# Sliding attention and a GEGLU block on one core: attention instructions over two token tiles, low weight parts by adding DMAs, kept x operands, weight loads issued by GpSimd

## The chip, the cores and the metric

The kernel runs on one core of a Trainium2 chip. The metric is the device time of one execution in microseconds (us). Five engines work from queues of their own: TensorE (PE) for matmuls, VectorE (DVE), ScalarE (ACT), GpSimd (POOL), and SyncE (SP), which here only issues DMAs. Each engine takes its instructions in order.

## The reference

With 2048 tokens, D = 512, 32 heads of 16, a feed-forward width of 1792 and all values in float32:

```
q, k, v = split(x @ wqkv)                      # 32 heads of 16
logits[s, w] = q[s] . k[s - 2 w] / 4           # w = 0..7; positions before 0 masked
a = (softmax(logits) @ v[s - 2 w]) @ wo
b = (gelu(x @ w_gate) * (x @ w_up)) @ w_down   # tanh form of gelu
g = sigmoid(sum(x * gate_w))
out = g * a + (1 - g) * b
```

## The kernel before

**Precision.** PE multiplies in float32r. Each operand is split into a high part (ACT copies it into float32r) and a low part, the raw value minus the high part; three products (high-high, high-low, low-high) replace one. The helper `split` (L64 to L69) does this: the copy at L68, the subtraction at L69, on whichever engine it is given.

**Parities.** A token only attends to tokens of its own parity, so the tokens are dealt into even and odd (`par` 0 and 1), 1024 each, in 8 tiles (`NP`) of 128.

**Projection.** `load_cb` brings in wqkv columns in three blocks (`cb`), `load_xk` and `load_x1` bring in x, and `project` multiplies them for each parity (L177). ACT or DVE evicts PSUM (`take`, L187, L189), and SP stores q, k and v to DRAM (`ks`, `qs`, `vs`).

**Attention** is DVE work. A generator, `attention`, goes through 8 units (parity, then 8 heads each), and in each through `scores`, `softmax` and `mix`. `scores` multiplies, tile by tile, 8 shifted k rows with q into `prod` (L238, 1024 elements per partition) and sums over the 16 values of a head (L239). POOL masks the result with `affine_select` (L242), for which `softmax` waits. `mix` multiplies v with the weights (L273), then folds 8 rows to one in three additions (L277, L278, L279) and transposes four tiles (L283); SP stores that to DRAM as `os`. The generator yields a cost after each group of instructions, and `pull(budget)`, called between pieces of the matrix work, draws as much as its budget allows. So these costs and budgets, and then a scheduler that reorders within dependencies, decide where attention stands between the other instructions of DVE.

**FFN.** For each parity, 14 chunks of 128 hidden columns (`FC`, loop in `ffn`). `gate_up` computes gate and up of two token blocks by seven products instead of eight, from sums of x blocks (`s1` to `s4`, made by `sums`, L114 to L117) and sums of weight blocks (`t1` to `t4`, made by `combine` at L344). The names `a11`, `a12`, `a22` are x blocks, `b11`, `b21`, `b22` weight blocks. `product` (L381) issues six matmuls. ACT and DVE take the results out (L385, L390, L466, L482), `hidden` multiplies gelu(gate) with up (L394) and splits (L396, L397; the subtraction is DVE's in parity 0 and POOL's in parity 1). `down` (L420) multiplies with w_down, two chunks at a time, one group behind.

**Weights of the FFN.** In parity 0, `fetch` loads a chunk's gate and up weights into `raw` from SP, `combine` makes the sums on DVE, and `operands` splits seven 256-column blocks into `w` tiles (ACT copy, POOL subtraction), each stored to DRAM as `ws`. `down_w` does the same for w_down (`d`, stored as `ds`). In parity 1 both are loaded back ready-made (`w<-ws`, `d<-ds`) by SP.

**x of the second parity.** At the end of parity 0's FFN, `operands_1` loads x again and makes sums and splits for the FFN of parity 1, with POOL doing the subtractions. `finish` multiplies attention's output, read back by `channels` in four DMAs per half, with wo (L557), scales and stores.

Tiles of `pool` with the same name share a fixed number of buffers (`BUFS`); a new tile waits until the readers of the oldest are done.

Of the kernel before, what the change touches and what calls it, by code (L numbers as in the profile page):

```python
# [33 lines left out]
OPS = ("b11", "t1", "t2", "b21", "b22", "t3", "t4")  # L34
# [3 lines left out]
def tile_gated_mix(ctx: ExitStack, tc: tile.TileContext, xt, wqkv, wff, wo, out):  # L38
# [6 lines left out]
    BUFS = {"A": 16, "S": 16, "w": 14, "d": 4, "raw": 2, "t": 1, "hh": 6, "hl": 6, "c": 4, "s": 3,  # L45
            "r": 2, "rt": 4, "p": 4, "lg": 2}
    COLS = {"w": 2 * WQ, "c": 2 * WQ, "d": 1024, "t": 1024, "raw": WT}

    def tl(tag, dt=F32):
        return pool.tile([P, COLS.get(tag, 512)], dt, name=tag, bufs=BUFS[tag])  # L50

# [20 lines left out]
    KS, VS, QS, OS, WS, DS = {}, {}, {}, {}, {}, {}  # L72
    for par in range(2):
        for hh in range(2):
            for n, t in (("k", KS), ("v", VS)):
                t[par, hh] = dram.tile([2, W + S // 2, UC], F32, name=f"{n}s{par}{hh}")
                for c in range(2):
                    nc.gpsimd.dma_start(t[par, hh][c, :W], zero)
            QS[par, hh] = dram.tile([2, S // 2, UC], F32, name=f"qs{par}{hh}")
        for u in range(NU):  # L80
            for half in range(2):
                OS[par, u, half] = dram.tile([32, 4, BT * P], F32, name=f"os{par}{u}{half}")


    early = iter(["c", "rt"] * 99)
    X, WC = {}, {}

    def load_xk(kc, blk, first=False):
        hi, lo = tl("A", F32R), tl("A", F32R)
        X[0, blk, kc] = hi, lo  # L90
        for a, n in ((0, P), (P, 512 - P)) if first else ((0, 512),):
            raw = tl(next(early))
# [4 lines left out]
    def load_cb(cb, kc, eng, tag=None):  # L97
        hi, lo = tl("w", F32R), tl("w", F32R)
        WC[cb, kc] = hi, lo
        raw = tl(tag or "c")  # L100
        if cb == 1:
            n = 2 * WQ
            for hh in range(2):
                nc.sync.dma_start(raw[:, hh * WQ:(hh + 1) * WQ], wqkv[hh, 2, :, kc * WQ:(kc + 1) * WQ])
        else:
            n = 512
            nc.sync.dma_start(raw[:, :n], wqkv[cb // 2, kc // 2, :, kc % 2 * 512:kc % 2 * 512 + 512])
        return lambda: split(eng, hi[:, :n], lo[:, :n], raw[:, :n])

    def sums(par, kc, a, b, eng, put, eng2=None):  # L110

        t = tl("t")
        s1, s2, s3, s4 = t[:, :512], t[:, 512:], b[:, :512], a[:, 512:1024]
        eng.tensor_tensor(s1, b[:, :512], b[:, 512:1024], op=OP.add)  # L114
        eng.tensor_tensor(s2, s1, a[:, :512], op=OP.subtract)
        eng.tensor_tensor(s3, a[:, :512], b[:, :512], op=OP.subtract)
        eng.tensor_tensor(s4, a[:, 512:1024], s2, op=OP.subtract)  # L117
        for n, s in (("s1", s1), ("s2", s2), ("s4", s4), ("s3", s3)):
            hi, lo = tl("S", F32R), tl("S", F32R)
            split(eng2 or eng, hi, lo, s)  # L120
            put(n, hi, lo)
            yield

    def raw_pair(par, kc):
        ab = []
        for blk in range(2):
            raw = tl("raw")
            nc.sync.dma_start(raw[:, :1024].rearrange("p (a c) -> p a c", a=2), xt[2 * par + blk, :, kc:kc + 3:2, :])
            ab.append(raw)
        return ab  # L130

    XOP, nxt = {}, {}

    def load_x1():
        for kc in range(2):
            a, b = raw_pair(1, kc)
            for blk, raw in ((0, a), (1, b)):
                for i in range(2):
                    if blk == 1 and (kc, i) != (1, 1):
                        d = tl("d", F32R)  # L140
                        hi, lo = d[:, :512], d[:, 512:]
                    else:
                        hi, lo = tl("hh", F32R), tl("hl", F32R)
                    X[1, blk, kc + 2 * i] = hi, lo
                    split(nc.vector, hi, lo, raw[:, i * 512:(i + 1) * 512])

    def operands_0():
        for kc in range(2):
            a, b = raw_pair(0, kc)
            for _ in sums(0, kc, a, b, nc.vector, lambda n, hi, lo: XOP.__setitem__((n, kc), (hi, lo))):  # L150
                pass
# [3 lines left out]
    def operands_1(first):  # L155
        for kc in range(2):
            a, b = raw_pair(1, kc) if kc else first
            for n, raw in (("a11", a[:, :512]), ("a12", a[:, 512:1024]), ("a22", b[:, 512:1024])):
                nxt[n, kc] = tl("A", F32R), tl("A", F32R)
                split(nc.gpsimd, *nxt[n, kc], raw)  # L160
                yield
            yield from sums(1, kc, a, b, nc.vector, lambda n, hi, lo: nxt.__setitem__((n, kc), (hi, lo)), nc.gpsimd)
# [69 lines left out]

    def scores(par, u):
        k, q = LG[par, u]
        lg = pool.tile([P, NP, W, UH], F32, name="lg", bufs=2)
        for jj in range(NP):
            prod = pool.tile([P, W, UC], F32, name="prod")
            nc.vector.tensor_tensor(prod, k[:, jj:jj + W, :], q[:, jj, None, :].to_broadcast([P, W, UC]), op=OP.mult)  # L238
            nc.vector.tensor_reduce(lg[:, jj].rearrange("p w h -> p (w h)"),  # L239
                                    prod.rearrange("p w (h d) -> p (w h) d", d=DH), axis=AX.X, op=OP.add)  # L240
            yield 2.5
# [21 lines left out]
    def mix(par, u):  # L263
# [4 lines left out]
        tb = pool.tile([P, NP, UC], F32, name="tb")  # L268
        for jj in range(NP):
            if jj % BT == 0:  # L270
                o = pool.tile([P, BT, UC], F32, name="o")
            prod = pool.tile([P, W, UC], F32, name="prod")
            nc.vector.tensor_tensor(prod.rearrange("p w (h d) -> p w h d", d=DH),  # L273
                                    v[:, jj:jj + W, :].rearrange("p w (h d) -> p w h d", d=DH),
                                    lg[:, jj, :, :, None].to_broadcast([P, W, UH, DH]), op=OP.mult)
            yield 1.2
            nc.vector.tensor_tensor(prod[:, :4], prod[:, :4], prod[:, 4:], op=OP.add)  # L277
            nc.vector.tensor_tensor(prod[:, :2], prod[:, :2], prod[:, 2:4], op=OP.add)  # L278
            nc.vector.tensor_tensor(o[:, jj % BT], prod[:, 0], prod[:, 1], op=OP.add)  # L279
            yield 1.4  # L280

            if jj % BT == BT - 1:
                nc.vector.transpose(tb[:, jj + 1 - BT:jj + 1].rearrange("p t c -> p (t c)"),  # L283
                                    o.rearrange("p t c -> p (t c)"))
                for a in range(4):
                    nc.sync.dma_start(OS[par, u, jj // BT][:, a], tb[32 * a:32 * a + 32, jj + 1 - BT:jj + 1])
# [44 lines left out]
    RAW = {}  # L331

    def fetch(f):
        raw = tl("raw")
        nc.sync.dma_start(raw[:, :1024], wff[f, :, :1024])
        RAW[f] = [raw]

    def combine(f):

        raw, t = RAW[f][0], tl("t")  # L340
        quart = raw[:, :1024].rearrange("p (a b) -> p a b", a=4)
        b11, b21, b12, b22 = (raw[:, i * 256:(i + 1) * 256] for i in range(4))
        t1, t3, t2, t4 = (t[:, i * 256:(i + 1) * 256] for i in range(4))
        sub = lambda o, a, b: nc.vector.tensor_tensor(o, a, b, op=OP.subtract)  # L344
        sub(t[:, :512].rearrange("p (a b) -> p a b", a=2), quart[:, 2:], quart[:, 0::2])
        sub(t2, b22, t1)
        sub(t4, b21, t2)
        RAW[f] = dict(b11=b11, b21=b21, b22=b22, t1=t1, t2=t2, t3=t3, t4=t4)

    def operands(par, f):  # L350

        WG[f] = {}
        if not par:
            WS[f] = dram.tile([len(OPS), P, 512], F32, name=f"ws{f}")
        for n in OPS if par else ("t1", "t2", "t3", "t4", "b11", "b21", "b22"):
            i = OPS.index(n)
            w = WG[f][n] = tl("w", F32R)
            if par:
                nc.sync.dma_start(w[:, :512].bitcast(F32), WS[f][i])
            else:  # L360
                split(nc.gpsimd, w[:, :256], w[:, 256:512], RAW[f][n])
                nc.sync.dma_start(WS[f][i], w[:, :512].bitcast(F32))
            yield

    def down_w(par, f):
        d = WD[f] = tl("d", F32R)
        if par:
            nc.sync.dma_start(d.bitcast(F32), DS[f])
            return
        rd = tl("r")  # L370
        nc.sync.dma_start(rd, wff[f, :, 1024:])
        DS[f] = dram.tile([P, 1024], F32, name=f"ds{f}")
        split(nc.gpsimd, d[:, :512], d[:, 512:], rd)
        nc.sync.dma_start(DS[f], d.bitcast(F32))

    def product(ps, a, w, start):
        for kc in range(2):
            ah, al = XOP[a, kc]
            wh, wl = w[:, kc * P:(kc + 1) * P], w[:, 256 + kc * P:256 + (kc + 1) * P]
# [13 lines left out]
    def hidden(key, ge, up, eng):  # L393
        nc.vector.tensor_tensor(ge, ge, up, op=OP.mult)  # L394
        hh_, hl_ = tl("hh", F32R), tl("hl", F32R)
# [36 lines left out]
    def gate_up(par, f, steps):  # L432
# [14 lines left out]

        X_ = bank("p")
# [13 lines left out]
        piece()  # L462
        idle(0.5)
# [7 lines left out]
        piece()  # L471
        product(X_, "s3", w["t3"], False)
# [3 lines left out]
        piece()  # L476
        idle(0.0)
# [7 lines left out]

    def ffn(par):
        for f in range(FC):
            def more():
                if f + 1 < FC:
                    for i, _ in enumerate(operands(par, f + 1)):  # L490
                        if i == 4 and not par and f + 2 < FC:
                            combine(f + 2)
                        yield
                else:
                    yield from load_o((0, 1), "w")
# [160 lines left out]
```

## Time and profile before

| what | value |
|---|---|
| median of 3 runs (lowest to highest) | 679.92 us (678.1 to 680.22) |
| profiled execution, its own time | 680.39 us |
| its span | 678.6 us, so 1.79 us lie around it |
| PE busy | 631.2 us (93%), 2839 matmuls |
| DVE busy | 584.4 us (86%), 714 instructions |
| ACT busy | 313.8 us (46%), 601 instructions |
| POOL busy | 236.1 us (35%), 198 instructions |
| mean granted TensorE clock | 0.967 |
| DMA | 136.46 MB, 116046 packets, 42400 of them under 512 B |

Matmuls are pipelined, so PE counts as busy when it is not full; the count of matmuls in a stretch tells more. The profile has the chain of waits, groups of instructions by line and shape (count, busy time, mean time of one, idle time ahead of them and what ended it), and, for any stretch of time, the busy time of every engine.

### The profile page before, as it was taken

To read this page: it belongs to the slowest core of one execution; us is meant where nothing else is said; L and a number is where in the kernel's file an instruction comes from. 1 tells how busy PE (TensorE), PEld (TensorE's weight loads), DVE (VectorE), ACT (ScalarE), POOL (GpSimd) and SP (SyncE) were. 2 spreads that over 40 slices of the span, in tenths; PEclk is the share of its full clock that TensorE was granted. 3 is DMA by queue.
4 is the path that set the end of the run, shared out by engine and by line. 5 is a ranking of instruction groups with operands and counts; after the bars stand their busy time and mean duration, and the time that the engine had idled before them with its cause. 6 is when DMAs were issued, how large, how long until landed. Compare 5 with 4: busy or idle time off the path is not lost.

```text
span 678.6 us, 8894 instructions
## 1 busy us (share of the span) xinstructions
PE 631.2 (93%) x2839; PEld 512.9 (76%) x2839; DVE 584.4 (86%) x714; ACT 313.8 (46%) x601; POOL 236.1 (35%) x198
## 2 busy tenths in 40 slices
PE   8998999996799979997989849999999999999997
PEld 6888998874587758875868637888777888887785
DVE  5439899879999999989999988998999999989432
ACT  4424442245446455655454564234434644454562
POOL 5204014066737364634471760023122221224220
PEclk9999999998799989998998978999999999999999
DMA  8885755597966665675457587776566766544163
GB/s 254 269 253 172 247 156 187 172 300 250 310 235 218 243 229 171 234 252 208 156 191 224 159 225 158 249 234 218 179 187 197 214 196 197 185 124 127 36 104 124
DMA packets 116046, 136.46 MB, mean 201 GB/s; under 512 B 42400, under 2 KB 68640, under 8 KB 116000
## 3 DMA queue, kind: packets, MB, share of 16 engines
q1 hardware_dynamic: 115488, 135.84, 63.8%
q8 instruction: 22, 0.36, 0.2%
q14 instruction: 24, 0.20, 0.1%
q0 software_dynamic: 512, 0.07, 0.1%
HBM read 81.80 MB, written 54.07 MB: 200 GB/s over the span
## 4 chain that ended last, share of the span: by engine, by line
DVE 41%; PE 38%; DMA 7%; issue 6%; ACT 4%; SPq 1%; POOL 1%; DVEq 0%; POOLq 0%; ACTq 0%
PE p L381 21%; DVE prod L273 6%; PE p L420 6%; PE acc L420 5%; DVE prod L238 5%; DVE prod L277 4%; DVE lg L239 4%; DMA raw<-xt 4%; PE acc L557 3%; PE p L557 3%; DVE t L344 3%; DVE c L394 3%; DVE c L390 2%; DVE prod L278 2%; DVE o L279 2%
## 5 line engine op out<-in xcount | busy, mean ns | idle before, releaser
L381 PE MATMUL p<-S,w 128*128 128x512 f32 x672 | 176.6, 406 | 10.2 <-DVE c L390 4.1
L381 PEld LDWEIGHTS p<-S,w 128*128 128x128 f32 x672 | 130.8, 195 | 42.8 <-DVE c L390 4.5
L381 PE MATMUL p<-A,w 128*128 128x512 f32 x504 | 135.6, 407 | 16.2 <-DVE c L390 16.0
L381 PEld LDWEIGHTS p<-A,w 128*128 128x128 f32 x504 | 97.1, 194 | 42.4 <-DVE c L390 20.0
L397 POOL TENSOR_TENSOR hl<-c,hh 128x512 fp32r<-128x512 f32 x28 | 44.7, 1595 | 168.5 <-ACT hh L396 141.4
L238 DVE TENSOR_TENSOR prod<-k,q 128x1024 f32<-128x1024 f32 x64 | 86.8, 1356 | 11.5 <-DMA q<-qs 10.6
L273 DVE TENSOR_TENSOR prod<-v,lg 128x1024 f32<-128x1024 f32 x64 | 81.5, 1273 | 6.7 <-DMA v<-vs 5.3
L420 PE MATMUL p<-d,hh 128*128 128x512 f32 x224 | 71.7, 405 | 10.5 <-ACT p L414 10.4
L239 DVE TENSOR_REDUCE lg<-prod 128x64 f32<-128x1024 f32 x64 | 77.7, 1214 | 1.1
L69 POOL TENSOR_TENSOR w<-t,w 128x256 fp32r<-128x256 f32 x56 | 58.4, 1056 | 48.2 <-ACT w L68 38.5
L396 ACT ACTIVATE hh<-c 128x512 fp32r<-128x512 f32 x56 | 35.3, 631 | 80.3 <-DVE c L394 80.0
L69 POOL TENSOR_TENSOR w<-raw,w 128x256 fp32r<-128x256 f32 x42 | 43.0, 1034 | 63.8 <-ACT w L68 60.6
L277 DVE TENSOR_TENSOR prod<-prod 128x512 f32<-128x512 f32 x64 | 59.0, 922 | 1.3
L420 PEld LDWEIGHTS p<-d,hh 128*128 128x128 f32 x224 | 43.0, 194 | 22.0 <-ACT p L414 11.8
L420 PE MATMUL acc<-d,hh 128*128 128x512 f32 x224 | 57.7, 394 | 0.7 <-ACT hh L396 0.7
L420 PEld LDWEIGHTS acc<-d,hh 128*128 128x128 f32 x224 | 41.8, 188 | 11.7 <-ACT hh L396 2.4
L394 DVE TENSOR_TENSOR c<-c 128x512 f32<-128x512 f32 x56 | 44.6, 796 | 5.2 <-ACT c L482 4.8
L385 ACT ACTIVATE s<-p 128x512 f32<-128x512 f32 x56 | 32.8, 593 | 26.2 <-PE p L381 26.2
L390 DVE TENSOR_TENSOR c<-p,s 128x512 f32<-128x512 f32 x56 | 38.0, 681 | 8.0 <-PE p L381 7.8
L420 PE MATMUL p<-d,hl 128*128 128x512 f32 x112 | 42.9, 394 | 0.0
L429 ACT ACTIVATE rt<-p 128x512 f32<-128x512 f32 x48 | 28.6, 595 | 29.4 <-PE p L420 28.0
L177 PE MATMUL p<-w,A 128*128 128x512 f32 (+2 forms) x192 | 38.5, 345 | 2.9 <-ACT w L68 1.1
(125 smaller groups left out, 1002.0 us busy)
## 6 DMA issues: line engine op xcount, KB each, us to landing
ws<-w SPq DMA_DIRECT2D x98, 256.0 KB, 2.9
w<-ws SPq DMA_DIRECT2D x98, 256.0 KB, 2.7
raw<-wff SPq DMA_DIRECT2D x14, 512.0 KB, 5.0
ds<-d SPq DMA_DIRECT2D x14, 512.0 KB, 3.9
d<-ds SPq DMA_DIRECT2D x14, 512.0 KB, 4.5
raw<-xt SPq DMA_DIRECT2D x12, 512.0 KB, 5.4
k<-ks SPq DMA_DIRECT2D x8, 512.0 KB, 5.0
q<-qs SPq DMA_DIRECT2D x8, 512.0 KB, 6.3
```

What stands on the lines that cost most here:

```text
L69: eng.tensor_tensor(lo, raw, hi.bitcast(F32), op=OP.subtract)
L177: nc.tensor.matmul(ps[:, :cn], a[:, t], w[:, c0:c0 + cn], start=(kc == 0 and n == 0), stop=(kc == KC - 1 and n == 2))
L238: nc.vector.tensor_tensor(prod, k[:, jj:jj + W, :], q[:, jj, None, :].to_broadcast([P, W, UC]), op=OP.mult)
L239: nc.vector.tensor_reduce(lg[:, jj].rearrange("p w h -> p (w h)"), prod.rearrange("p w (h d) -> p (w h) d", d=DH), axis=AX.X, op=OP.add)
L273: nc.vector.tensor_tensor(prod.rearrange("p w (h d) -> p w h d", d=DH), v[:, jj:jj + W, :].rearrange("p w (h d) -> p w h d", d=DH), lg[:, ...
L277: nc.vector.tensor_tensor(prod[:, :4], prod[:, :4], prod[:, 4:], op=OP.add)
L381: nc.tensor.matmul(ps, w_, a_, start=(start and kc == 0 and n == 0), stop=(kc == 1 and n == 2), skip_group_check=True)
L390: nc.vector.tensor_tensor(c, ps, s, op=OP.add)
L394: nc.vector.tensor_tensor(ge, ge, up, op=OP.mult)
L397: eng.tensor_tensor(hl_, ge, hh_.bitcast(F32), op=OP.subtract)
L420: nc.tensor.matmul(pp, a[:, ts], w, start=(i == 0 and n == 0 and gr == 0), stop=(i == 1 and n == 2), skip_group_check=True)
L557: nc.tensor.matmul(pa, a, b, start=False, stop=(u == NU - 1 and n == 2), skip_group_check=True)
```

## The change

Four things are changed, and buffers are laid out anew to make room.

1. **Two token tiles per instruction.** `scores` and `mix` work on two tiles at once: `prod` has 2048 elements, a view `spans` reads the two overlapping sets of 8 rows. Costs in `yield` are new. `o`, `tb` and `os` are laid out so that `channels` reads a half with one DMA in whole rows.
2. **Low weight parts by adding DMAs.** `operands` lets ACT write the negated high part into the low part's place, and a DMA issued by GpSimd adds the raw value to it in SBUF; then ACT writes the high part. The seven blocks and an unused quarter lie in one `raw` tile, so that there are two such steps per chunk (768 and 1024 columns). `combine` works in place.
3. **Both parities make their weights.** `ws` and `ds` are gone; `fetch`, `combine`, `operands` and `down_w` run for every chunk of both parities. `fetch` (two DMAs), `fetch_d` and wo's `fetch_o` are issued by GpSimd. `ahead` and `again` prepare the first chunks of parity 1 while parity 0 ends.
4. **x operands of parity 1 are kept.** `load_x1` also makes the sums and their splits, on DVE, at the start; `keep` and `keep_x1` store all of them to DRAM, 28 DMAs from GpSimd, and `operands_1` loads each back at the end of parity 0, 14 DMAs from GpSimd. Parity 0's output is also stored by GpSimd.

The core of the diff:

```diff
+GROUPS = (("t1", "t2", "b11"), ("b22", "t3", "t4", "b21"))
+QUARTS = ("t1", "t2", "b11", "b12", "b22", "t3", "t4", "b21")
...
+    def keep(n, kc, hi, lo):
+        x = XS[n, kc] = dram.tile([P, 1024], F32, name=f"x{n}{kc}")
+        nc.gpsimd.dma_start(x[:, :512], hi.bitcast(F32))
+        nc.gpsimd.dma_start(x[:, 512:], lo.bitcast(F32))
...
+            for n, x in sums(a, b):
+                hi, lo = pair("S")
+                split(nc.vector, hi, lo, x)
+                keep(n, kc, hi, lo)
...
-        for jj in range(NP):
-            prod = pool.tile([P, W, UC], F32, name="prod")
-            nc.vector.tensor_tensor(prod, k[:, jj:jj + W, :], q[:, jj, None, :].to_broadcast([P, W, UC]), op=OP.mult)
...
-            yield 2.5
+        for jj in range(0, NP, 2):
+            prod = pool.tile([P, 2, W, UC], F32, name="prod")
+            nc.vector.tensor_tensor(prod, spans(k, jj), q[:, jj:jj + 2, None, :].to_broadcast([P, 2, W, UC]), op=OP.mult)
+            yield 2.3
...
+            yield 2.3
...
     def fetch(f):
-        raw = tl("raw")
-        nc.sync.dma_start(raw[:, :1024], wff[f, :, :1024])
-        RAW[f] = [raw]
+        raw = RAW[f] = tl("raw")
+        r = raw.rearrange("p (a c) -> p a c", c=QW)
+        q = wff[f, :, :1024].rearrange("p (a c) -> p a c", c=QW)
+        nc.gpsimd.dma_start(r[:, 2::5], q[:, :2])
+        nc.gpsimd.dma_start(r[:, 3:5], q[:, 2:])
...
-    def operands(par, f):
-        for n in OPS if par else ("t1", "t2", "t3", "t4", "b11", "b21", "b22"):
-            i = OPS.index(n)
-            w = WG[f][n] = tl("w", F32R)
-            if par:
-                nc.sync.dma_start(w[:, :512].bitcast(F32), WS[f][i])
-            else:
-                split(nc.gpsimd, w[:, :256], w[:, 256:512], RAW[f][n])
-                nc.sync.dma_start(WS[f][i], w[:, :512].bitcast(F32))
+    def operands(f):
+        for i, ops in enumerate(GROUPS):
+            n = len(ops) * QW
+            w = tl(f"g{i}", F32R)
+            hi, lo = w[:, :n], w[:, n:2 * n]
...
+            raw = RAW[f][:, (0, 4)[i] * QW:][:, :n]
+            nc.scalar.activation(lo, raw, AF.Copy, scale=-1.0)
+            nc.gpsimd.dma_start(lo.bitcast(F32), raw, accum_op=OP.add)
+            yield
+            nc.scalar.activation(hi, raw, AF.Copy)
+            yield
...
-    def down_w(par, f):
+    def down_w(f):
         d = WD[f] = tl("d", F32R)
-        if par:
-            nc.sync.dma_start(d.bitcast(F32), DS[f])
-            return
...
+        split(nc.gpsimd, d[:, :512], d[:, 512:], RD.pop(f))
...
     def channels(par, u, half):
         o = tl(("r", "rt")[half])
-        src = OS[par, u, half].rearrange("i a (t b j) -> b i (a t) j", t=BT, b=4)
-        for b in range(4):
-            nc.sync.dma_start(o[32 * b:32 * b + 32].rearrange("p (m j) -> p m j", j=32), src[b])
+        nc.sync.dma_start(o, OS[par, u, half].rearrange("b i a c -> (b i) (a c)"))
```

More of the change, by code (lines that the diff above doesn't have):

```diff
@@ L446, in piece, with anew @@
                 down(par, *s)
+        def anew(*names):
+            if not par and f == FC - 1:
+                for n in names:
+                    operands_1(n)
         X_ = bank("p")
@@ L484, in gate_up, with ahead, again @@
         late.append(last)
+    AGAIN = {}
+    def ahead():
+        combine(0)
+        AGAIN[0] = operands(0)
+        for _ in range(2):
+            yield next(AGAIN[0])
+    def again():
+        yield from AGAIN.pop(0)
+        yield from load_o((2, 3), (tl("c", F32R)[:, :512] for _ in range(4)))
+        fetch(1)
+        yield
+        combine(1)
     def ffn(par):
@@ L598, in tile_gated_mix @@
     combine(0)
-    ops = operands(0, 0)
-    for i in range(6):
-        next(ops)
+    for _ in operands(0):
+        pass
     combine(1)
```

273 lines of the change are left out of this document (159 added, 114 removed).

## The prediction

> **What bounds the kernel now.** I read the 40 slices first (PE nearly full at both ends, thinner in the middle, DVE at 9 there), then the chain of waits (DVE 41%, PE 38%), then the table of stretches. I cut it where the list of DVE's instructions has landmarks: the first `prod` of L238 (44.67), the first `c` of L390 in either parity's FFN (161.74 and 443.95) and that of chunk 10 of the second (591.91). I call the stretches A, B, C, D1, D2. After the columns come PE, PEld, DVE, ACT, POOL busy, granted clock, DMA share, GB/s.
>
> ```profile
> core 0: us, PE busy (x) PEld busy (x) DVE busy (x) ACT busy (x) POOL busy (x), PEclk, DMA share, GB/s
> 0.00:44.67 44.67, 42.48 (x195) 34.28 (x196) 16.58 (x29) 19.30 (x32) 12.48 (x23) 1.00 0.88 266
> 44.67:161.74 117.07, 109.20 (x648) 96.10 (x647) 108.00 (x132) 42.55 (x111) 33.19 (x26) 0.99 0.65 203
> 161.74:443.95 282.21, 250.48 (x1016) 198.69 (x1016) 267.59 (x322) 146.82 (x286) 136.54 (x115) 0.93 0.68 221
> 443.95:591.91 147.96, 147.75 (x637) 118.96 (x636) 140.75 (x166) 64.36 (x105) 34.22 (x23) 1.00 0.63 199
> 591.91:678.60 86.69, 81.30 (x349) 64.85 (x347) 51.43 (x69) 40.80 (x69) 19.68 (x13) 1.00 0.40 103
> ```
>
> A full PE takes 88 matmuls of 512 columns in 20 us (the slice 560 to 580), 0.227 us each. C has 1016, so PE needs 231 us and gets 282: C is DVE's, busy 95% of it. D1 needs 637 x 0.227 = 145 of 148: PE's, with DVE (95% busy) close behind. D2 is PE's. PE's queue says the same of C: its largest idle time there is 19.0 us behind DVE's `c` of L390.
>
> Why DVE is slow in C: the same instruction costs more beside POOL. Alone, L277 takes 0.69 us; beside POOL's subtraction, 1.11 and 1.64.
>
> ```profile
> 129.19 0.69 DVE L277 TENSOR_TENSOR prod<-prod 128x512 f32<-128x512 f32 x1
> ...
> 147.93 1.11 DVE L277 TENSOR_TENSOR prod<-prod 128x512 f32<-128x512 f32 x1
> 148.46 2.82 POOL L69 TENSOR_TENSOR w<-raw,w 128x256 fp32r<-128x256 f32 x3
> ...
> 151.24 2.25 POOL L69 TENSOR_TENSOR d<-r,d 128x512 fp32r<-128x512 f32 x1
> 152.39 1.64 DVE L277 TENSOR_TENSOR prod<-prod 128x512 f32<-128x512 f32 x1
> ```
>
> Over C, forms with two SBUF inputs are stretched and the reduction is not (1.21 us in every stretch):
>
> ```profile
> L397 DVE TENSOR_TENSOR hl<-c,hh 128x512 fp32r<-128x512 f32 x28 | 27.1, 967 | 3.4 <-ACT hh L396 3.3
> L277 DVE TENSOR_TENSOR prod<-prod 128x512 f32<-128x512 f32 x27 | 24.4, 903 | 0.4
> L239 DVE TENSOR_REDUCE lg<-prod 128x64 f32<-128x1024 f32 x25 | 30.2, 1209 | 0.2
> ```
>
> Mean less time alone (1.23 us for 1024 elements, 0.69 for 512, 0.42 for 256, 0.29 for 128), times count, over all such forms of C gives **47 us of collisions**, for 136.5 us of POOL work. In D1 it gives 11, in B 11.
>
> **The change, part by part.** The list of the built kernels' instructions, engine by engine as the scheduler leaves them, has no times; I price it with times alone (2048 elements: 2 x 1.23 - 0.16 = 2.29; a line through 0.42, 0.69 and 1.23 gives 1.04 ns an element and 0.16 fixed).
>
> DVE alone, before and after: A 17.8 and 32.3; B 103.3 and 97.4; C 239.6 and 245.6; D1 136.8 and 145.3; D2 46.6 and 21.0. In all 544 and 542: hardly less. Two token tiles in one instruction take 192 of 384 instructions away, 192 x 0.16 = -30 us. But `combine` now runs in both parities, 14 x (0.69 + 2 x 0.42) = +21, and eight low parts of the second parity's sums come from POOL, +6. Attention also moves forward: the budgets in `yield` shrink less than the work, so C holds 159 us of it (before 151), D1 102 (109), D2 none (27). So what can be gained is collisions, and it comes where POOL's work goes.
>
> *A and B.* The sums and their low parts fill time in which DVE idles (16.6 of 44.7 busy). The first `prod` waits for `q`, which waits for SP; two `raw` loads of the first parity now stand on SP ahead of the `ks`/`qs` stores and wait for DVE, and 28 DMAs of 256 KB (`keep`, 7.3 MB) join a DMA that is 88% busy. 7.3 MB at 266 GB/s is 27 us if all of it were in the way, nothing if none; stores and loads there are about 2 MB, 8 us, and sharing doubles that at most. I take **+5** (0 to 12). B: 97.4 alone, collisions from 11 to 3 (POOL keeps four column splits and an `affine_select`); independent neighbours start about 0.09 us before the end of the one before, some 0.05 us per instruction, -4; idle as before, 9 (6 of it one wait for `v`): 105 for 117, **-12**.
>
> *C.* POOL loses 81 splits of `w` (82 us) and 14 of `A` and `S` (23), and keeps `d`, four of `wo` and selects, 34 us: collisions 47 x 34/136.5 = 12. Overlap -0.06 x 253 = -15 (before -0.06 x 320 = -19, which closes 239.6 + 47 - 19 = 267.6). Idle as before, 14.6. 245.6 + 12 - 15 + 14.6 = 257 for 282: **-25**. PE's 231 stays under it.
>
> *D1.* `d` is split on POOL here too (before, a load): 12 x 1.75 us beside 34, so collisions 11 x 55/34 = 18, overlap -9, idle 6 (before 7): 145.3 + 18 - 9 + 6 = 160 for 148: **+12**. Before, PE bounded this stretch by 3 us; now DVE does.
>
> *D2* is PE's either way; without attention the `ACT hh` and `os` waits ahead of the last `hl` (11 us of DVE idle, PE 81 of 87) shrink: **-1**, 0 to -4. `os` read in rows of 2 KB by one DMA instead of four in rows of 128 B is part of that.
>
> *ACT* gets per chunk two copies of 768 and two of 1024 elements; its rows (256: 0.41, 512: 0.63) give 0.84 and 1.06, so 3.8 us where the first parity had 7 x 0.41 = 2.9 and the second none, and `d`'s 0.63 is new in the second. D's ACT goes from 45% to about 70%. Nothing, as long as DVE and PE bound; without that cover each copy of 1.06 can stand ahead of a PSUM copy that PE waits for.
>
> *SP and DMA.* `ws` and `ds`, both ways 65 MB of 136, go; adding DMAs (25 MB, which also read what they write), weights in both parities and `x` come, at most 75 MB. At 0.68 and 0.63 share that is hidden.
>
> *POOL's queue* is the unknown: five DMAs per chunk (two loads of quarters, two adding, one of `d`), in one line with `d`, `hl` and the selects. A load of quarters waits until the adding DMA two places ahead has read its buffer. The trace has only DMAs of 8 rows from POOL:
>
> ```profile
> 3.58 1.03 POOL L78 DMA_DIRECT2D ks<-zero  x2
> ```
>
> that is 0.52 us each; with 128 rows between that and 16 times it. I take 1.0, near the row. Landing: 512 KB took 3.9 (`ds`) to 5.0 (`wff`); an adding DMA lies between 3.9 and twice 5.0, I take 4. POOL's period in D1 is then 3.1 (`hl`) + 1.75 + 5 + 4 = 14, under 16: nothing. The Trainium skill ("DMA: Bandwidth & Descriptors", Anatomy of one DMA) gives DMAs from GpSimd 2.0 us plus bytes/436 GB/s: an estimate of 2.9 and 3.2 us to land, a period of 13, and a rival below that would decide from 1.6 us of issue; no run here shows it yet.
>
> **Sum**, against the profiled execution (680.39, span 678.60, 1.79 around it; the median of three runs is 679.92): +5 - 12 - 25 + 12 - 1 = -21. Softmax stands behind POOL's selects (before 2.2 us of waits in all); POOL's line now holds waits for landings, and six selects at 0.5 more give +3. So -18: span 660.6, **662 us**.
>
> **Rivals.** *PE becomes the bound (faster).* If collisions in D1 do not grow and C comes near PE's 231 (say 240, since the adds PE waits for come sooner): -7 - 42 + 0 - 1: 630. For: PE's granted clock is 0.93 in C and 1.00 elsewhere, after idle times of 2.7 to 7.7 us. Against: DVE alone has 245.6 in C. The clock has a rule in the Trainium skill ("TensorE: Matmul & The Clock Gate", Part 1): an idle window of about 3.4 us halves it, so shorter gaps would restore it; the trace agrees (0.69 in 400 to 420, with a 7.7 us gap). By it alone C's PE time falls but DVE's stays, and the sum does not change.
>
> *POOL's line becomes the bound (slower).* One DMA at i us of issue: D1's period of 16 is passed from i = (16 - 3.1 - 1.75 - 4)/5 = 1.4. At 2 us it is 18.9, and 12 full chunks cost 2.9 each, +35: 697; the same at 4 us of landing and 1.4 more of it. For: nothing shows a DMA of 128 rows there. Against: 1.4 is 2.7 times the row.
>
> *The gain is given back (no change).* The list of DVE hardly shrinks; if the head is late by 12 and selects and adding DMAs hold DVE or ACT by 1 us a chunk, +7 + 14: 679 to 683. Speaking for it: DVE's 95% in C and D1 leaves nothing to absorb waits.
>
> **Chances.** Forecast (650 to 674) 0.48; PE bound 0.2; given back (674 to 684) 0.1; POOL bound 0.22. Measurement tells 0.3%, 2 us, from no change. Faster 0.48 + 0.2 + 0.03 = 0.71, same 0.05, slower 0.24. The range leaves out a tenth at each end: 638 (half of the PE case) to 692 (half of the POOL case).
>
> **What would show it.** Right: C at 250 to 265 us with L277's successor near 1.3 us, D1 at 155 to 165 with DVE above 95%, D2 without attention, first `prod` by 50. Wrong: POOL waiting for landings with DVE behind its selects; `prod` after 57; DMAs on POOL above 1.4 us; a merged `prod` (4-dimensional operands) far from 2.29 us.

## The result, and the profile after

The changed kernel takes **691.31 us** (median of 4, 690.01 to 691.69) where the kernel before, measured beside it, takes 679.27: a ratio of 1.0175, 95% interval 1.0151 to 1.0198. It is slower by 1.75%; the forecast was 662 us, faster. The profiled execution has a span of 689.9 us.

The table of stretches of the kernel after, cut at the same landmarks (now the `prod` of L288 and the `c` of L442; columns as before):

```profile
0.00:63.20 63.20, 58.40 (x289) 48.45 (x290) 35.04 (x50) 26.17 (x45) 28.79 (x52) 0.97 0.95 309
63.20:172.10 108.90, 98.53 (x561) 86.76 (x560) 94.13 (x87) 41.31 (x96) 19.98 (x22) 0.95 0.70 198
172.10:442.01 269.91, 242.89 (x1012) 191.70 (x1011) 238.67 (x255) 162.81 (x255) 107.69 (x124) 0.97 0.68 185
442.01:604.74 162.73, 153.91 (x639) 122.63 (x638) 153.68 (x150) 97.75 (x153) 86.88 (x75) 0.97 0.52 128
604.74:689.90 85.16, 80.87 (x346) 64.43 (x344) 24.02 (x33) 43.65 (x74) 25.65 (x23) 1.00 0.33 93
```

| | A | B | C | D1 | D2 | span |
|---|---|---|---|---|---|---|
| before | 44.7 | 117.1 | 282.2 | 148.0 | 86.7 | 678.6 |
| forecast | 49.7 | 105.1 | 257.2 | 160.0 | 85.7 | 660.6 with 3 for selects |
| after | 63.2 | 108.9 | 269.9 | 162.7 | 85.2 | 689.9 |

The span misses by 29.3: A and B together by 17.4, C by 12.7, D1 by 2.7, D2 by -0.5, less the 3 for selects. The two large terms are what has to be explained.

In A the DMA is nearly full: share 0.95, against 0.88 before; at 309 GB/s it moves 19.5 MB in A, where before it moved 11.9 (266 GB/s for 44.7 us). VectorE's largest wait in A is not for `q` but for a load of x: its list has one pair of the first parity's sums (L150) ahead of the first scores.

```profile
59.20 0.69 DVE L150 TENSOR_TENSOR raw<-raw 128x512 f32<-128x512 f32 x1 [13.23 <-DMA raw<-xt]
...
63.21 2.29 DVE L288 TENSOR_TENSOR prod<-k,q 128x2048 f32<-128x2048 f32 x1 [0.60 <-DMA q<-qs]
```

In C, VectorE is busy 238.67 us, against 242.6 in the forecast (245.6 + 12 - 15); it is idle 31.2 us, against 14.6. The groups of VectorE in C, by shape (before, L277 took 903 ns, two to a pair; the reduction 1209):

```profile
L288 DVE TENSOR_TENSOR prod<-k,q 128x2048 f32<-128x2048 f32 x16 | 36.5, 2280 | 0.1
L290 DVE TENSOR_REDUCE lg<-prod 128x128 f32<-128x2048 f32 x16 | 36.5, 2279 | 0.0
...
L449 DVE TENSOR_TENSOR hl<-c,hh 128x512 fp32r<-128x512 f32 x28 | 21.8, 778 | 3.6 <-ACT hh L448 3.6
...
L328 DVE TENSOR_TENSOR prod<-prod 128x1024 f32<-128x1024 f32 x14 | 17.1, 1219 | 0.1
```

They stand at nearly their times alone (2.29, 1.23; `hl` 778 ns where it was 967): most of the collisions are gone, as forecast. What came is waiting. VectorE's waits in C (what waits, for what; us in all, times, longest):

```profile
DVE raw L402 <- DMA raw<-wff: 11.0, 8, 3.0
DVE m L306 <- ACT lg L305: 6.8, 4, 2.8
DVE m L301 <- POOL lg L293: 6.6, 2, 6.2
```

The first is `combine`, reached before its load has landed. One hole of TensorE, at the turn to the second parity, shows a longer chain of the same kind, in the timeline of after:

```profile
413.14 5.65 POOL L76 TENSOR_TENSOR d<-r,d 128x512 fp32r<-128x512 f32 x1 [1.27 <-ACT d L75]
...
419.09 0.55 POOL L396 DMA_DIRECT2D r<-wff  x1 [0.30 <-POOL d L76]
419.65 1.27 POOL L76 TENSOR_TENSOR d<-r,d 128x512 fp32r<-128x512 f32 x1
...
425.32 0.63 ACT L75 ACTIVATE d<-r 128x512 fp32r<-128x512 f32 x1 [8.84 <-DMA r<-wff]
425.85 1.04 ACT L418 ACTIVATE g<-raw 128x1024 fp32r<-128x1024 f32 x1
426.80 1.04 ACT L421 ACTIVATE g<-raw 128x1024 fp32r<-128x1024 f32 x1
...
428.37 2.93 PE L433 MATMUL p<-A,g 128*128 128x512 f32 x6 [9.97 <-ACT s L660]
```

Read it downwards: POOL's subtraction of `d`, 1.27 us the next time, takes 5.65; the next load of `d` is issued behind it; ScalarE waits 8.84 us for that load, with two weight copies and the PSUM copy (L660) queued behind, and TensorE waits 9.97 us for the last of them. Why 5.65 is seen in VectorE's timeline:

```profile
413.15 0.68 DVE L76 TENSOR_TENSOR hl<-rt,hh 128x512 fp32r<-128x512 f32 x1
413.75 1.02 DVE L402 TENSOR_TENSOR raw<-raw 128x512 f32<-128x512 f32 x2
414.69 2.29 DVE L288 TENSOR_TENSOR prod<-k,q 128x2048 f32<-128x2048 f32 x1
416.89 0.76 DVE L402 TENSOR_TENSOR raw<-raw 128x256 f32<-128x256 f32 x2
417.56 2.28 DVE L290 TENSOR_REDUCE lg<-prod 128x128 f32<-128x2048 f32 x1
```

Two-input instructions stand back to back until the reduction at 417.56, and POOL ends 1.23 us after that, at 418.79. The Trainium skill ("SBUF — State Buffer", Who interferes with whom) says that a VectorE instruction with two SBUF inputs contends with POOL's reads and that a reduction does not; the trace agrees, 1.23 us being nearly all of the subtraction's 1.27.

### The profile page after: what moved, and what is told of

It is laid out like the page before. It is cut to its first block, busy times and chain, and to the rows that moved or that the text cites. A ratio compares the mean times of both kernels' runs of the same rounds, so it can differ in the third digit from the quotient of the medians.

```text
span 689.9 us, 8271 instructions
## 1 busy us (share of the span) xinstructions
PE 634.6 (92%) x2839; PEld 514.0 (74%) x2839; DVE 545.5 (79%) x572; ACT 371.7 (54%) x623; POOL 269.0 (39%) x294
## 4 chain that ended last, share of the span: by engine, by line
PE 41%; DVE 21%; DMA 18%; issue 11%; POOL 3%; ACT 3%; SPq 2%; DVEq 0%; POOLq 0%; ACTq 0%
PE p L433 24%; PE acc L472 8%; PE p L472 6%; DMA raw<-wff 5%; DMA raw<-xt 4%; DVE prod L324 3%; DVE raw L402 2%; DVE prod L328 2%; DMA g<-raw 2%; DMA r<-wff 2%; DVE prod L288 2%; DVE c L446 2%; DVE c L442 2%; DVE lg L290 2%; PE acc L649 2%
## 5 line engine op out<-in xcount | busy, mean ns | idle before, releaser
L433 PE MATMUL p<-S,g 128*128 128x512 f32 x672 | 172.2, 399 | 9.3 <-ACT p L508 4.1
L433 PEld LDWEIGHTS p<-S,g 128*128 128x128 f32 x672 | 127.5, 191 | 41.4 <-ACT p L508 5.8
L433 PE MATMUL p<-A,g 128*128 128x512 f32 x504 | 134.7, 404 | 21.1 <-DVE c L442 11.1
L433 PEld LDWEIGHTS p<-A,g 128*128 128x128 f32 x504 | 95.5, 192 | 48.1 <-DVE c L442 15.8
L419 POOL DMA_DIRECT2D g<-raw x56 | 50.2, 896 | 171.3 <-ACT g L418 156.9
L324 DVE TENSOR_TENSOR prod<-v,lg 128x2048 f32<-128x2048 f32 x32 | 75.1, 2348 | 5.6 <-DMA v<-vs 5.1
L288 DVE TENSOR_TENSOR prod<-k,q 128x2048 f32<-128x2048 f32 x32 | 73.8, 2306 | 1.3 <-DMA q<-qs 1.2
L402 DVE TENSOR_TENSOR raw<-raw 128x256 f32<-128x256 f32 (+1 forms) x84 | 55.8, 666 | 22.5 <-DMA raw<-wff 21.7
L290 DVE TENSOR_REDUCE lg<-prod 128x128 f32<-128x2048 f32 x32 | 72.9, 2279 | 0.1
L449 POOL TENSOR_TENSOR hl<-c,hh 128x512 fp32r<-128x512 f32 x28 | 46.6, 1683 | 34.7 <-ACT hh L448 34.5
L418 ACT ACTIVATE g<-raw 128x1024 fp32r<-128x1024 f32 (+1 forms) x56 | 53.1, 949 | 12.0 <-DVE raw L402 9.9
L442 DVE TENSOR_TENSOR c<-p,s 128x512 f32<-128x512 f32 x56 | 37.8, 680 | 23.2 <-PE p L433 23.1
L391 POOL DMA_DIRECT2D raw<-wff x28 | 21.1, 755 | 89.8 <-DVE S L76 34.1
L472 PEld LDWEIGHTS acc<-d,hh 128*128 128x128 f32 x224 | 44.1, 198 | 14.2 <-ACT hh L448 3.9
L421 ACT ACTIVATE g<-raw 128x1024 fp32r<-128x1024 f32 (+1 forms) x56 | 52.9, 944 | 0.0
```

What stands on the lines that cost most here:

```text
L288: nc.vector.tensor_tensor(prod, spans(k, jj), q[:, jj:jj + 2, None, :].to_broadcast([P, 2, W, UC]), op=OP.mult)
L290: nc.vector.tensor_reduce(lg[:, jj:jj + 2].rearrange("p j w h -> p (j w h)"), prod.rearrange("p j w (h d) -> p (j w h) d", d=DH), axis=AX. ...
L324: nc.vector.tensor_tensor(prod.rearrange("p j w (h d) -> p j w h d", d=DH), spans(v, jj).rearrange("p j w (h d) -> p j w h d", d=DH), lg[: ...
L418: nc.scalar.activation(lo, raw, AF.Copy, scale=-1.0)
L419: nc.gpsimd.dma_start(lo.bitcast(F32), raw, accum_op=OP.add)
L421: nc.scalar.activation(hi, raw, AF.Copy)
```

## The experiments

All are measured beside the kernel before (677.8 to 679.0 us in these comparisons). Stretches are those above, in us of the profiled execution.

| | median | ratio to before | A | B | C | D1 | D2 |
|---|---|---|---|---|---|---|---|
| e1 pairs | 672.00 | 0.9887-0.9939 | 43.1 | 115.0 | 274.9 | 149.0 | 86.3 |
| e2 no keep | 681.35 | 1.0022-1.0066 | 46.6 | 110.9 | 273.1 | 163.4 | 85.3 |
| e3 SP loads | 702.58 | 1.0346-1.0396 | 62.4 | 115.2 | 275.8 | 165.6 | 84.3 |
| e4 weights back | 668.15 | 0.9818-0.9900 | 63.6 | 106.0 | 263.7 | 148.1 | 84.7 |
| e5 late d | 688.82 | 1.0123-1.0185 | 61.8 | 106.9 | 266.0 | 166.6 | 85.2 |
| e6 late combine | 686.72 | 1.0084-1.0167 | 61.5 | 106.4 | 267.2 | 163.1 | 86.3 |
| e7 x1 late | 688.22 | 1.0085-1.0165 | 68.8 | 105.8 | 261.8 | 166.6 | 83.6 |
| e8 d on DVE | 672.73 | 0.9876-0.9945 | 62.1 | 106.6 | 256.1 | 161.5 | 84.7 |
| e9 hold | 672.45 | 0.9856-0.9929 | 61.8 | 107.3 | 258.0 | 159.4 | 84.0 |
| e10 head | 682.50 | 1.0030-1.0086 | 45.6 | 123.7 | 268.0 | 158.0 | 85.2 |
| e11 hold, pace | 677.54 | 0.9951-1.0016 | 61.9 | 107.2 | 263.0 | 157.2 | 89.8 |
| e12 sorted | 663.89 | 0.9749-0.9794 | 46.2 | 124.6 | 258.8 | 147.4 | 84.6 |
| e13 held | 674.75 | 0.9925-0.9975 | 62.8 | 104.9 | 253.9 | 166.1 | 86.9 |
| e14 x at turn | 656.30 | 0.9648-0.9728 | 45.5 | 110.1 | 268.7 | 144.3 | 84.3 |
| e15 x, sorted | 655.74 | 0.9633-0.9707 | 44.4 | 107.9 | 268.5 | 147.3 | 84.2 |
| e16 x, held | 657.17 | 0.9647-0.9716 | 44.1 | 109.4 | 271.1 | 147.2 | 84.3 |
| e17 x, held, sorted | 647.22 | 0.9484-0.9580 | 46.6 | 104.7 | 266.1 | 144.8 | 84.3 |
| e18 no keep, held | 670.28 | 0.9847-0.9928 | 47.9 | 108.1 | 256.3 | 167.8 | 84.9 |

**e1: part 1 alone, on the kernel before.**

```diff
-        for jj in range(NP):
+        for jj in range(0, NP, 2):
```

> Part 1 alone on the kernel before: two token tiles per attention instruction, with the new os layout (tb is one tile per half, for room). Theory (DVE's work bounds B and C): 192 fewer instructions take 0.16 us each off DVE, B some 8 us and C some 15 us shorter, D1 within 3 us: 655 to 662 us. Rival (longer instructions stand ahead of the adds PE waits for): PE's idle time behind DVE's c grows and the time stays at 675 to 685.

It gained 6 us, between the two theories: C fell by 7 only, as POOL's splits of `w` still collide there (L243's `prod` took 2437 ns, where after has 2306). What the rival names is seen too, if small: TensorE waits 21.5 us in C for the adds of PSUM and `s` (19.0 before).

**e2: without 26 of the 28 stores of kept operands.**

```diff
+        if (n, kc) != ("a11", 0):
+            return
...
-            nc.gpsimd.dma_start(t.bitcast(F32), XS[n, kc])
+            nc.gpsimd.dma_start(t.bitcast(F32), XS["a11", 0])
```

> The changed kernel with 2 of the 28 stores of x operands; all 14 loads at the end of the first parity read the one that is stored, so the second parity's FFN computes with wrong x (the work left out is 26 stores of 256 KB). Theory (the stores fill the DMA at the head and hold the first prod): first prod from 63 to about 50 us, total down by 10 to 13: 678 to 681 us. Rival (SP blocked by the raw loads that wait for DVE holds it): first prod stays above 58, total 687 to 691.

A falls by 16.6 and the time by 10. The row of A, with a DMA share of 0.81 for 0.95, and its first scores:

```profile
0.00:46.60 46.60, 43.83 (x202) 35.01 (x203) 30.14 (x45) 24.61 (x42) 15.96 (x26) 1.00 0.81 250
```
```profile
46.62 2.29 DVE L290 TENSOR_TENSOR prod<-k,q 128x2048 f32<-128x2048 f32 x1 [7.56 <-DMA q<-qs]
```

VectorE's list changed with it: the pair of sums that waited 13.23 us in after now stands behind the first scores. So e2 alone does not part the bytes from this order; e10 does.

**e3: weight loads from SyncE again.**

```diff
-        nc.gpsimd.dma_start(RD[f], wff[f, :, 1024:])
+        nc.sync.dma_start(RD[f], wff[f, :, 1024:])
```

(so too the other weight loads).

> The changed kernel with the loads of FFN weights and wo issued by SP again. Theory (GpSimd's line delays the loads that ACT's copy of d waits for): the hole of PE at 418 to 440 us shrinks by about 8 us and waits of ACT's d copy for r<-wff fall from 25 us below 8: 678 to 684 us. Rival (the copy stands too early in ACT's list whoever issues): waits and time as before, 688 to 692.

Both theories fell; it is 11 us slower. SyncE, in order, now waits 180.4 us in all for adding DMAs to free `raw`, with attention's loads and stores behind it. Issuing these loads from GpSimd is no loss in this kernel.

**e4: weights made once.** Parity 0 stores its finished parts, parity 1 loads them.

```diff
+            if (f, i) in WS:
+                nc.sync.dma_start(w[:, :2 * n].bitcast(F32), WS[f, i])
...
+            nc.sync.dma_start(WS[f, i], w[:, :2 * n].bitcast(F32))
```

> The changed kernel with parts 1, 2 and 4, but in the second parity all FFN weights are loaded ready-made from DRAM, as in the kernel before (stored by SP in the first parity). Theory (D1 is longer because combine and the subtraction of d load DVE and collide with it): D1 from 163 back to 148 to 151, total 676 to 680 us. Rival (D1 is longer because attention instructions are coarser): D1 stays at 160 or more, total 688 or more.

D1 is TensorE's again, 148.1 with VectorE busy 118 (13 us of that relief is attention that its list now has in C); 23 us in all, 14.6 of them in D1.

**e5 to e7: three moves in the program text.**

```diff
-            down_w(f)
             steps = []
...
+            down_w(f)
             for _ in bg:
```

> The kernel after, but the split of a chunk's down weights (ScalarE's copy of d and POOL's subtraction) is put at the end of its chunk, not ahead of its first product. Theory: in the kernel after ScalarE's copy of d waits for its load in line ahead of the PSUM copies that TensorE needs (23.1 us of waiting in all, 8.8 us of it at the turn to the second parity, where TensorE has a hole of 10.0 us). Then stretch C falls by 8 to 12 us, the wait of the copy of d for its load goes under 3 us, and the kernel takes 679 to 684 us. Rival: VectorE's list decides C anyway, and the hole is only the place where it shows; VectorE waits elsewhere instead, for POOL's select (6.2 us there before): 687 to 692 us.

```diff
+                if 0 < f < FC - 1:
+                    combine(f + 1)
...
-                if f + 2 < FC:
-                    combine(f + 2)
```

> The kernel after, but VectorE's sums of a chunk's quarters (combine) are put at the start of the chunk ahead of it, not at the end of the one before that, so that their load has about one third of a chunk more to land. Theory: VectorE's waits for the loads of the quarters (11.0 us in C, 2.7 in D1), which come because such a load must wait on POOL until the adding DMA two chunks back has landed, are idle time of a list that is otherwise full: C falls by 8 to 11, D1 by 2, the kernel takes 677 to 682 us. Rival: the weights are then late for the products, ScalarE's copies wait for VectorE's sums, and TensorE for both: C and D1 stay within 3 us, 688 to 694 us.

```diff
     project(1, 0)
+    sums_x1()
+    project(0, 1)
     operands_0()
-    project(0, 1)
     keep_x1()
```

> The kernel after, but the sums of the second parity's x and their 16 stores are made behind the projection of values of that parity, from a second load of x (2 MB), and the first parity's sums one projection later. Theory: the first scores come late because stores of 4 MB stand in the head, where the DMA is full (0.99 share): A falls from 63.2 to 47 to 52, B grows by what VectorE makes there instead (sums and low parts, 11 us, part of it in idle time), the kernel takes 679 to 684 us. Rival: the work and the bytes are the same and only shift from A to B and C, 688 to 692 us; A falls but B and C grow as much.

None tested its theory. In e5 and e6 the built list of VectorE is that of after, instruction by instruction (lists of other engines moved a little, and with them the time by 2 to 5 us), and in e7 the 16 stores still stand in the head, beside more loads: 22.6 MB in A, where after has 19.5, and A grows by 5.6. The program text alone does not set the order. Where a later experiment holds something back, it does so with an edge of issue alone (`tc.issue_after`).

**e8: `d` on VectorE.**

```diff
-        split(nc.gpsimd, d[:, :512], d[:, 512:], RD.pop(f))
+        split(nc.vector, d[:, :512], d[:, 512:], RD.pop(f))
```

> The kernel after, but the low part of d (a subtraction of 512 elements in every chunk) is made on VectorE, not on POOL. Theory: collisions cost what they did in the forecast's sum (in D1 18 us for 55 us of POOL work in two-input instructions, 0.33 us for each), so VectorE gains 0.33 x 1.76 = 0.6 us a chunk and pays 0.69: D1 stays within 2 us of 162.7, C within 5 of 269.9, the kernel takes 687 to 695 us. Rival: POOL's line (loads, adding DMAs and their landings, subtractions) sets the period of D1; with 1.76 us less a chunk D1 falls by 10 us or more and the kernel takes 674 to 682 us.

18.6 us faster than after, a little more than the rival has; but the gain is in C (-14), not in D1 (-1). Its list had also changed: 18 us of attention, at times alone, now came in D2, where VectorE has room. So:

**e9: that order, `d` on POOL.**

```diff
-            c = next(fill, None)
+            with (tc.issue_after(LAST[-1]) if LAST else ExitStack()):
+                c = next(fill, None)
```

> The kernel after, but each piece of attention is queued on VectorE behind the add of PSUM and s (c) that the program text has ahead of it (an order of issue alone; the scheduler had moved pieces ahead of such adds). The list of the built kernel then has, in instructions of attention at their times alone, 149 us in C (after: 156), 91 in D1 (101), 18 in D2 (0); e8, which made the low part of d on VectorE, had 144, 96 and 18. Theory (order): e8 gained because its list leaves 18 us of attention for D2, where VectorE idles, not because POOL's line became shorter. Then this kernel, with d on POOL as in after, has C at 259 to 264, D1 at 151 to 156 and takes 670 to 677 us. Rival (POOL): the subtraction of d on POOL stretches the two-input instructions and delays loads; with it back in place the time is that of after, 685 to 692 us.

The theory of order holds: 672.45 against e8's 672.73. Where `d` is subtracted makes no difference that can be seen; where attention stands does. (The edge holds every piece of attention, so it is this order as a whole that is shown, not the 18 us alone.) The rows of C, D1 and D2 (VectorE is 9 and 6 us less busy than in after in C and D1, and 20 more in D2):

```profile
169.13:427.13 258.00, 241.76 (x1011) 190.44 (x1010) 229.28 (x247) 160.23 (x252) 103.46 (x121) 0.99 0.68 187
427.13:586.50 159.37, 152.39 (x642) 120.70 (x641) 147.37 (x141) 100.85 (x156) 84.01 (x80) 0.99 0.57 140
586.50:670.50 84.00, 79.66 (x342) 64.18 (x342) 43.97 (x50) 44.29 (x75) 24.29 (x20) 1.00 0.35 95
```

**e10: the stores behind the first scores.**

```diff
+    with tc.issue_after(HOLD["sel"]):
+        for x in SUMS:
+            keep(*x)
+        keep_x1()
+    with tc.issue_after(HOLD["q"]):
+        operands_0()
```

> The kernel after, but all 28 stores of x operands are queued on POOL behind the first affine_select, and the two pairs of raw loads of the first parity's sums on SyncE behind the first load of q (order of issue alone). Theory: the head is late by the 7.3 MB of stores and 2 MB of loads that stand ahead of the first scores; A falls from 63.2 to 45 to 50, B takes the bytes beside its work (DMA share 0.73 there) and grows by 3 us at most, the kernel takes 672 to 678 us. Rival: POOL's line of 28 stores (0.5 to 0.9 us each) holds the next select and column splits, B grows by 8 to 12, 682 to 688 us. (e7 said nothing on this: its list of issue still had the 16 stores ahead of the first scores, and 3 MB more of loads.)

A is as early as the theory has it, and the time is the rival's: B takes 14.8 more. A + B is 169.3 (after 172.1, e2 157.4), with the DMA share of B at 0.82 for 0.70. In B a store of `v` is late to land, ScalarE's next copy waits for its buffer, and the copy for a sum of x, queued behind it, holds VectorE:

```profile
94.74 0.38 ACT L234 ACTIVATE s<-p 128x256 f32<-128x256 f32 x1 [9.76 <-DMA vs<-s]
```
```profile
95.68 0.69 DVE L76 TENSOR_TENSOR S<-raw,S 128x512 fp32r<-128x512 f32 x1 [7.18 <-ACT S L75]
```

The stores cost wherever they stand: 12 us of A + B against e2, with the load of x held behind the first load of `q`. The other 6 of the 9 us that e10 gains on after are in C to D2, where 7 us less of attention is left.

**e11, e12: more of attention held back; all parts together.**

```diff
-            yield 2.3
+            yield 2.5
```

> As e9, and the budgets in the yields of attention are those of before for the same work (2.5, 2.5, 2.5, 1.4, 1.3): attention at its times alone is 139 us in C, 80 in D1, 38 in D2. Theory (order): C 249 to 255, D1 145 to 148 (then TensorE's), D2 85 to 88, the kernel takes 655 to 664 us. Rival: D2 pays what C and D1 gain, since the last projection needs all of attention; D2 grows by 10 or more and the kernel takes 668 us or more.

```diff
-            pull(n)
+            pull(n * 1.15 if par else n * 0.85)
```

> All parts that helped in one kernel: e4 (the second parity loads ready-made parts), e10's head, e9's order with the budgets of the FFN's stretches times 0.85 in the first parity and 1.15 in the second: attention at its times alone is 137 us in C, 96 in D1, 22 in D2. Theory: the causes are separate and add up: A 46 to 50, B 104 to 108, C 238 to 248 (TensorE's 231 is near), D1 148 (TensorE's), D2 85 to 87: 625 to 638 us. Rival: with less of VectorE's work C is held by ScalarE's line (weight copies ahead of PSUM copies) instead, and stays above 255: 645 us or more.

e11 has its rival's time, but not by its rival's cause: D2 pays 4.6 where that had 10, and C does not follow. With VectorE busy 227.8 there, C is still 263: VectorE then waits 23.5 us for `raw`. e12 is 664, not 625 to 638: B holds the stores, and C stays at 259 with VectorE busy only 215.6. Its rival has the number; that ScalarE's line is the cause is not shown.

**e13: the two waits held out of the way in C.**

```diff
+                    with tc.issue_after(LAST[-1]):
+                        combine(f + 1)
...
+            with tc.issue_after(GE[-1]):
+                down_w(f)
```

> The kernel after, but each chunk's sums of quarters are queued on VectorE behind the last add of the chunk before the one that needs them, and ScalarE's copy of d behind that chunk's Gelu (order of issue alone; e5 and e6 had moved the same two in the program text, and the scheduler put VectorE's list back as it was). VectorE's list keeps 154, 101 and 1 us of attention in C, D1 and D2 (after: 156, 101, 0), so it has as much to do as in after. Theory: the idle time that the forecast lacked in C (31 against 14.6 us) is waits of an order in which VectorE meets loads that have not landed (13.7 us in C and D1) and ScalarE meets d's load (23.1): C falls by 10 to 14, D1 by 2 to 4, the kernel takes 672 to 680 us. Rival: the waits move to others of the same chain (ScalarE's weight copies behind VectorE's sums, TensorE behind those): C and D1 together fall by less than 5, the kernel takes 684 to 692 us.

The theory holds for C: 16 us less with as much work, and its idle time, 17.7, is near the forecast's 14.6. D1 gives 3 back, and B is 4 shorter. Both pieces were held at once, so the share of each is not known. The row of C, and VectorE's wait for the load (11.0 in after):

```profile
167.66:421.52 253.86, 240.75 (x1014) 192.49 (x1012) 236.17 (x253) 160.46 (x252) 102.49 (x117) 0.98 0.69 191
```
```profile
DVE raw L403 <- DMA raw<-wff: 1.6, 1, 1.6
```

**e14: e4 with x made at the turn, nothing of it stored.**

```diff
-                keep(n, kc, hi, lo)
...
+            for _ in operands_1():
+                pass
```

> As e4 (the second parity loads ready-made weight parts), but the second parity's x operands are made at the turn, from a second load of x (2 MB), with low parts on POOL, and nothing of them is stored (7.3 MB written and 7.3 MB read less). Theory: those bytes cost 12 to 18 us of A and B wherever they stand (e10 moved them from A to B, and A + B stayed at 169.3 against 172.1, where e2 without them had 157.4); A + B comes to 156 to 160, C grows by 0 to 4 for the sums at the turn, the kernel takes 653 to 660 us. Rival: the operands at the turn hold TensorE until they are made, as the turn has 33 us of down and output products at most beside 8 sums, 14 copies and 14 low parts: C grows by 8 or more, 664 us or more.

The theory holds: A + B 155.7, 12 us less in all than e4; C grows by 5, one more than it gave.

**e15 to e17: what is left in C.** e15 adds e9's order to e14, e16 e13's two edges, e17 both; the edits are those shown there, with the budgets that the expectations name.

> As e14, with e9's order and the budgets of e12 (0.85 in the first parity, 1.15 in the second): attention at its times alone is 121 us in C, 107 in D1, 22 in D2 (e14: 153, 93, 0). Theory: with A + B at 156 to 160, C at 250 to 255 (VectorE has 32 us less to do there, but e11 and e12 showed C near 258 with VectorE waiting), D1 148, D2 85: 640 to 650 us. Rival: C does not fall below 262, as the DMA (0.96 share in e12's C) or ScalarE's line holds it: 653 us or more.

> As e14, with e13's two pieces (sums of quarters behind the last add of the chunk before, copy of d behind the Gelu). VectorE's list keeps e14's attention (152, 91 and 0 us in C, D1, D2; e14: 153, 93, 0). Theory (C's excess is waits of the order of issue, as e13 showed on the kernel after): C falls from 269.3 to 254 to 260, A + B and D stay, the kernel takes 641 to 649 us. Rival: with 281 GB/s of DMA in C (after: 185) the loads and the stores of weight parts set C's pace, held order or not: C above 265, 652 us or more.

> As e16, with e9's order of attention and budgets of 0.92 and 1.1: attention at its times alone is 134 us in C, 95 in D1, 21 in D2. Theory: with the waits gone VectorE's list decides C again, and 18 us less of it makes C 240 to 248 (TensorE's 231 is near), D1 148, D2 85: 630 to 640 us. Rival: without the attention that filled it VectorE waits again, as in e11, e12 and e15, and the time is that of e16 within 4 us.

e15's theory fell, and so did e16's: in e16 TensorE now waits 7.5 us in C for adding DMAs to land. The issues of DMA in C, first of after, then of e16 (KB each, median us to landing):

```profile
g<-raw POOLq DMA_DIRECT2D x14, 512.0 KB, 4.8
raw<-wff POOLq DMA_DIRECT2D x28, 256.0 KB, 4.2
```
```profile
g<-raw POOLq DMA_DIRECT2D x12, 512.0 KB, 7.3
raw<-wff POOLq DMA_DIRECT2D x20, 256.0 KB, 7.3
```

Beside the stores of weight parts (279 GB/s in C, 185 in after) both land 2.5 to 3 us later, and a chunk waits for a load, then for an adding DMA. That this chain sets C at 266 to 271 is argued from these rows, not shown by a run. Against it, in e17 TensorE waits only 2.5 us for adding DMAs, and C is still 266; and VectorE's largest wait in C of e16 is 12.9 us for ScalarE's exponential (L300), so ScalarE's line is a rival that no run sets apart. e17 is the fastest of all, 647.22 us (ratio 0.9532), 7 over its theory's range and below its rival's.

**e18: e2 and e13 together.**

> e2 and e13 in one kernel: as in e2, all but one of the x operands are left out of the 28 stores and every load of the second parity reads that one (its second parity computes from wrong x operands), and as in e13 the sums of quarters and the copy of d are held back in the order of issue. Theory: the stores' bytes and the order in C are the two terms that the forecast lacked, and they add: 691.3 - 10.0 (e2) - 16.6 (e13) = 664.7, so 661 to 668 us, with A + B at 156 to 160 and C at 253 to 258; that is near the forecast's 662. Rival: they share the same waits (a head without stores lets the same work pile up in C), and the kernel stays at 670 us or more.

The times fall into two groups, 666.2 to 668.7 and 671.8 to 675.7, with a median of 670.3, on the rival's edge; the profiled execution is of the first (666.6), and what parts the groups is not known. By stretches the terms add: A + B 156.0 and C 256.3, against the forecast's 154.7 and 257.2. D1, at 167.8, is 5 over after and 8 over the forecast: VectorE is busy 159.3 us there (153.7 in after) with no more attention to do, as collisions, reckoned as in the prediction, are 25 us there for 18.

## Why the prediction was wrong

- **A, +5: the step that failed first.** It let the 7.3 MB of `keep` cost no more than a sharing with some 2 MB of the head's own traffic. The head gave up 18.5 us, and even its upper end was 12; the first `prod` at 63.2 is past the 57 that was to show it wrong. A and B have to be taken together: e2 and e14 have 157.4 and 155.7, near the forecast's 154.7, so the stores of `keep` are the miss, 14 to 15 us of A + B (e2 against after, e14 against e4) and 10 to 12 us of the whole time. e10 shows that B has no room for them either: with the stores and that load of x moved out of A, A + B gave back only 3.
- **B, -12:** measured -8.2; without the stores -6 to -7 (e2, e14), and A then +1 to +2 for +5. Their sum is right, the split is not.
- **C, -25: the idle term was mis-sized**, 31.2 us for "idle as before, 14.6", a term taken over from a kernel without this chain of loads, sums and landings. Its other terms came out: by the groups, reckoned as in the prediction, collisions are 10 us (forecast 12), busy time 238.7 (242.6). The prediction took ScalarE's copies, GpSimd's queue and the landings as hidden; they are hidden on average, but VectorE and ScalarE met them in an order fixed ahead, and stood. e13 took that away and C was 253.9, inside the 250 to 265 given.
- **D1, +12, and D2, -1: right** (+14.7, -1.5). Collisions in D1 are 18 us by the groups, as forecast; VectorE, 94% busy, decides. e4 shows what making the weights again costs the whole kernel: 23 us.
- **Selects, +3:** VectorE waits 9.1 us for them in all of B, C and D1 (2.2 before); 6.2 of that is the hole at the turn.
- **Small prices right:** the merged `prod` 2.306 (2.29), GpSimd's issue of an adding DMA 0.90 (1.0), its landing 4.6 to 4.7 (4). The estimate in the prediction from the Trainium skill ("DMA: Bandwidth & Descriptors", Anatomy of one DMA), 2.9 and 3.2 for that landing, is not borne out.
- **Rivals.** POOL's line as the bound of D1 did not come (e8, e9); that its 697 lies nearest the measured 691 is luck. "Given back" named the head and waits of about a us per chunk and was nearest in kind, but at 679 to 683 too small. PE as the bound did not come.

As a sum of parts, from runs that lie side by side: pairs and adding DMAs, with weights made once and x at the turn, give 656.3 (-22 from before); keeping x early costs 12 (e4), making the weights again 23 (after). The parts depend on the order in which they are added: from after itself, e2 gives the stores 10.

## What to carry to other kernels

Where an engine's order is fixed ahead, count each landing that it meets in line, not only the busy times: taking the waits for one load and one copy out of line was worth 16 us here. Bytes added where the DMA is already 0.88 busy cost time, and moving them to a stretch at 0.70 gave back only 3 of the 15 us (A + B of e10 and of e2 against after). Before an edit that moves something is believed or dismissed, look whether the built list of instructions moved at all.

## What the runs showed of the hardware

- An adding DMA (SBUF to SBUF, issued by GpSimd) took 0.90 us of issue; 384 and 512 KB landed after 4.6 and 4.7 us, and after 7.2 and 7.3 us in C of e16, where the DMA moved 279 GB/s.
- A subtraction on POOL stood nearly still, in the one place looked at, as long as VectorE ran two-input instructions back to back: 5.65 us for 1.27.
- The DMA in the head moved 309 GB/s at a share of 0.95, and 329 at 0.99 in e7.
